# Pooled attention and a two-layer mixer on one core: lambda and alpha1 loaded to all partitions, in place of spreading them by products

## The chip, the core and the metric

The kernel runs on one core of a Trainium2 chip. The metric is the device time of one execution in microseconds (us), the median of several runs. The core has five engines with instruction streams of their own: TensorE (PE; its weight loads are shown apart as PEld), VectorE (DVE), ScalarE (ACT), GpSimd (POOL) and SyncE (SP). SP and ACT issue transfers on hardware queues (q1 and q10 in the profile), POOL on the software queue (q0), which also converts types on the way. All queues are served by the same 16 DMA engines.

## What is computed

For each of 8 batches and 8 heads, 576 tokens of width 64 attend to 72 keys and values, each the mean of 8 neighbouring ones; the heads side by side make x (576 x 512 per batch). Then a mixer works on x: along the tokens, and along the channels through a hidden layer of 2048.

```python
k_p = k.reshape(B, H, Sp, pool, D).mean(axis=3)   # v_p likewise; pool = 8
attn = softmax(q @ k_p.T / sqrt(D))
x = attn @ v_p                                    # heads side by side: (8, 576, 512)
a1 = alpha1 * x + beta1
tok = einsum('ts,bsd->btd', w_tok, a1)
u = x + lam * tok
a2 = alpha2 * u + beta2
out = u + lam * (maximum(a2 @ w_ch1, 0) @ w_ch2)
```

## The kernel before

All order is written out by hand: the schedule of the framework is off, and each engine works through its instructions in the order of the code. The outermost unit is a block of four token chunks of 128 rows (nine blocks). While PE does the channel mixer of block n (`mlp_A`, then `mlp_B` or `product`), the attention of batch n + 1 and its token mixer (`mix_T`) are put between its products, by lists of due times. Nothing of that part is touched. The change lies in what comes before the first block: the constants, the loads of batch 0, its attention, and the transposes of `w_tok`.

**Folding of the vectors.** The kernel multiplies x by `lamal_bc` = lambda * alpha1 (`att_X` L765 and `rest_X` L758) before the token product; beta1 * lambda is one more row of the moving operand (`bias_row`, L471). So it needs lambda and lambda * alpha1 in all 128 partitions, as `lam_bc` and `lamal_bc`. Before, lambda (two rows), beta1 (two rows) and alpha1 (one row) are loaded as rows of a tile `vecs` (L397, L405). PE spreads a row over the partitions by a product of a row of ones with it in fp32: `spread_lam` (L491, 512 columns, which ACT copies to `lam_bc`), and `spread_al1` twice (L498, 256 columns each, which DVE multiplies by `lam_bc` into `lamal_bc`, L499).

**The first loads.** SP issues half of `rem_raw` (the last 64 tokens of q and k), beta1 and alpha2; ACT issues lambda, the other half of `rem_raw`, alpha1 and beta2; POOL issues, on the software queue and in this order, q of heads 0 to 3, k of heads 0 to 3, v (L300, L295), then k, q and v of heads 4 to 7, `w_tok` (L381, L385) and `w_ch1` (L555). The software queue delivers them in that order.

**Attention of batch 0.** `att_F` transposes q on PE (L589), `att_Frem` the rest of q. `double_k` copies a quarter of k on DVE (L620) and casts the rest of k (L365, L366). `att_K` pools k by 16 products (L632) and 4 on the rest (L638); ACT and then DVE take the two halves out to `kpT` (L648). `att_S` makes the scores and ACT their exponentials; `first_V` pools v; `att_AV` multiplies by v, and DVE divides (L749, L751) into `x_tm`. `att_X` and `rest_X` make `xs`, on POOL or DVE. `double_k`, `cast_rem`, `more_constants` (four memsets, L479 to L482) and the evictions all stand on DVE, in code order.

**Weights of the token mixer.** `setup_wtok(i)` transposes a fifth of `w_tok` on PE (L516), and ACT copies it to `wtT` (L519). `setup_rowsum(i)` adds up its columns on PE (L528), and ACT casts the row into `wtT` (L530). `setup_vectors` transposes beta2 and alpha2 (L503, three small ACT copies). `mix_T(0, 0)` (L801) is the first token product; it needs the first fifth of `wtT`, its sum, and all of batch 0's `xs`. DVE adds x (L805), POOL or DVE multiplies by alpha2 (L811), PE transposes (`mix_uT`, L825), and `mlp_A` (L849) begins.

**Unread products.** `keep_warm(n)` (L792) issues n products of 512 columns whose result nobody reads.

The tile `vecs` lends its place later to scaled `w_ch2` weights; its size per partition stays.

Of the kernel before, what the change touches and what calls it, by code (L numbers as in the profile page):

```python
# [7 lines left out]
FP = mybir.dt.float32  # L8
# [3 lines left out]
ALU = mybir.AluOpType  # L12
AX = mybir.AxisListType

P = 128
SPG = 72
DM = 512
# [171 lines left out]
def direct(  # L189
# [28 lines left out]
    def gp(name):  # L218
        return psA.tile([P, 512], FP, tag="gp", name=name)
# [171 lines left out]

    vecs = const.tile([65, 3, DM], FP, tag="vecs", name="vecs")
    ones_row = const.tile([1, P], FP, tag="ones_row", name="ones_row")
    nc.vector.memset(ones_row, 1.0)

    def load_vector(i, src, queue=nc.scalar):
        queue.dma_start(out=vecs[0:65:64, i], in_=src.unsqueeze(0).to_broadcast((2, DM)))  # L397

    new_batch(0)
    load_vector(0, moe_lam)  # L400
    load_rem(0)
    load_q_bf(0, 0)
    load_k16(0, 0)
    load_vector(1, moe_beta1, nc.sync)
    nc.scalar.dma_start(out=vecs[0:1, 2], in_=moe_alpha1.unsqueeze(0))  # L405
    start = const.tile([1, 2], FP, tag="start", name="start")
# [47 lines left out]
    for i in range(2):  # L454
# [6 lines left out]
    nc.vector.memset(pool_vr, 0.0)  # L461
    nc.vector.memset(vr16, 0.0)
    nc.vector.tensor_scalar(out=pool_v[:, 0:64], in0=pool_main, scalar1=8.0, scalar2=None,
                            op0=ALU.mult)
# [4 lines left out]
    def bias_row(i):  # L469
        p0 = 64 - 64 * i  # L470
        nc.vector.tensor_tensor(out=xs_pool[i][p0:p0 + 1, 4, :], in0=vecs[p0:p0 + 1, 1],  # L471
                                in1=vecs[p0:p0 + 1, 0], op=ALU.mult)

# [4 lines left out]
    def more_constants():  # L478
        nc.vector.memset(ones_bf, 1.0)  # L479
        nc.vector.memset(ones_lo[0:64], 1.0)  # L480
        nc.vector.memset(ones_lo[64:128], 0.0)
        nc.vector.memset(wtT[:, :, S:640], 0.0)  # L482

    def load_al2(behind):
        behind.memset(al2_bc[:, 0:1], 0.0)
        nc.sync.dma_start(out=al2_bc, in_=moe_alpha2.unsqueeze(0).to_broadcast((P, DM)))

    def spread_lam():

        ps = gp("ps_bc")  # L490
        nc.tensor.matmul(out=ps, lhsT=ones_row, rhs=vecs[0:1, 0])  # L491
        nc.scalar.copy(out=lam_bc, in_=ps)

    def spread_al1(half):

        ps = gp("ps_bc")[:, 0:256]
        cols = slice(256 * half, 256 * half + 256)
        nc.tensor.matmul(out=ps, lhsT=ones_row, rhs=vecs[0:1, 2, cols])  # L498
        nc.vector.tensor_tensor(out=lamal_bc[:, cols], in0=lam_bc[:, cols], in1=ps, op=ALU.mult)  # L499

# [287 lines left out]
    def keep_warm(count):  # L788

        ps = psB.tile([P, DM], FP, tag="ch", bufs=2, name="ps_warm")  # L790
        for _ in range(count):
            nc.tensor.matmul(out=ps, lhsT=warm[:, 0:P], rhs=warm)  # L792
# [209 lines left out]
    cast_rem(0, nc.vector)  # L1002
    more_constants()
    keep_warm(1)
    att_Frem(0, nc.scalar.copy)
    keep_warm(1)
    spread_lam()
    double_k(0)
    att_K(0, 0, None)
    spread_al1(0)  # L1010
    bias_row(0)
# [6 lines left out]
    att_S(0, 3)  # L1018
    att_AV(0, 1)
    att_K(0, 1, nc.scalar.copy)  # L1020
    att_F(0, 2, nc.vector.tensor_copy)
    late_copy = att_F(0, 3, None)
    att_AV(0, 2)
    att_X(0, 0, 2, nc.gpsimd, False)
    att_AV(0, 3)
# [8 lines left out]
    att_S(0, 6)  # L1034
    spread_al1(1)
    att_AV(0, 5)
# [4 lines left out]
    load_rem(1, behind=nc.vector)  # L1041
    keep_warm(1)
    setup_wtok(1, nc.scalar.copy)
    keep_warm(1)
    att_AV(0, 7)
    keep_warm(1)
    setup_rowsum(0)
    setup_wtok(2, nc.scalar.copy)
    rest_X(0, 4, 6, nc.gpsimd)
    load_w1(1)  # L1050
    setup_wtok(3, nc.scalar.copy)
    setup_rowsum(1)
    setup_vectors()
    setup_wtok(4, nc.scalar.copy)
# [199 lines left out]
```

## Time and profile before

| what | us |
|---|---|
| median of 3 runs (332.32 to 332.98) | 332.51 |
| the profiled execution | 332.4 |
| its span in the profile | 330.7 |
| PE busy | 325.0 |
| DVE / ACT / POOL busy | 236.6 / 175.6 / 95.4 |

The page gives, for one execution, each engine's busy time and the chain of work that ended last. The chain is followed back from the last instruction: at each step to what released it, or to the instruction before it on its engine. A step on the chain counts with the time by which the chain moves on; the timeline counts an instruction's whole duration, which with pipelined products is longer. "Landing" is the time from a DMA's issue to the last update of its semaphore, and the trace has it for POOL's DMAs alone. The view by stages gives each engine's busy time, the granted clock and the GB/s moved in stretches of the span.

### The profile page before, as it was taken

The numbers are of one execution on the slowest core, as the hardware profiler recorded it, in microseconds if no ns is written. First come the engines' busy times: TensorE is split into PE (matmuls) and PEld (weight loads), VectorE is DVE, ScalarE is ACT, GpSimd is POOL, SyncE is SP. The second block draws the span as 40 slices with busy tenths as digits, with TensorE's granted clock in tenths as the row PEclk, the third lists the DMA queues.
The fourth block names the chain that finished last, engine by engine and source line by source line (L and its number), as shares of the span: only waits on it lengthen the run. The fifth ranks groups of instructions, "written<-read, shape, count | busy, mean of one in ns | idle before, by whom it ended". The sixth has DMA issues, their size and how long they took to land.

```text
span 330.7 us, 6526 instructions
## 1 busy us (share of the span) xinstructions
PE 325.0 (98%) x2531; PEld 209.1 (63%) x2531; DVE 236.6 (72%) x490; ACT 175.6 (53%) x322; POOL 95.4 (29%) x110
## 2 busy tenths in 40 slices
PE   8999999999999999999999999999999999999995
PEld 3667764455545576656775677557755866586584
DVE  7774389999589969776967696878688783265263
ACT  3775989368323852387128812782268225803710
POOL 8769736501256011700290028102610200000000
PEclk9999999999999999999999999999999999999999
DMA  8999999958895982399549934995340044003003
GB/s 122 185 218 265 268 209 249 219 145 114 171 258 65 227 199 60 74 235 162 161 116 205 171 122 89 211 196 152 65 136 2 0 65 143 2 0 128 3 32 97
DMA packets 66618, 45.83 MB, mean 139 GB/s; under 512 B 34541, under 2 KB 57205, under 8 KB 66586
## 3 DMA queue, kind: packets, MB, share of 16 engines
q1 hardware_dynamic: 52236, 32.67, 42.4%
q0 software_dynamic: 13824, 12.40, 23.3%
q8 instruction: 20, 0.33, 0.4%
q10 hardware_dynamic: 526, 0.34, 0.4%
q14 instruction: 12, 0.10, 0.1%
HBM read 38.30 MB, written 9.44 MB: 144 GB/s over the span
## 4 chain that ended last, share of the span: by engine, by line
PE 97%; DVE 1%; POOL 0%; issue 0%; ACT 0%
PE ps_h L849 38%; PE ps_w L972 26%; PE ps_tok L801 11%; PE ps_ch L869 8%; PE ps_av L743 3%; PE ps_s L700 2%; PE ps_warm L792 2%; PE ps_kp L632 1%; PE ps_r L707 1%; PE ps_av L747 1%; PE ps_q L589 1%; PE ps_sc L680 0%; PE ps_w L516 0%; DVE u_sb L805 0%; POOL u_bf L811 0%; PE ps_v L659 0%
## 5 line engine op out<-in xcount | busy, mean ns | idle before, releaser
L849 PE MATMUL ps_h<-u_fm,w 128*128 128x512 bf16 (+2 forms) x608 | 133.7, 369 | 0.2 <-DVE bias_cols L852 0.2
L856 ACT ACTIVATE H<-ps_h,bias_cols 128x512 bf16<-128x512 f32 x144 | 98.2, 688 | 55.4 <-PE ps_h L849 54.5
L849 PEld LDWEIGHTS <-w 128*128 128x128 bf16 x608 | 65.8, 114 | 49.7 <-issue 2.2
L972 PEld LDWEIGHTS <-H 128*128 128x128 bf16 x560 | 53.4, 98 | 10.8 <-DVE u_sb L990 1.2
L809 ACT CAST u_bf<-u_sb 128x512 bf16<-128x512 f32 x32 | 19.8, 618 | 71.2 <-issue 39.9
L972 PE MATMUL ps_w<-w_l,H 128*128 128x256 bf16 x448 | 53.6, 273 | 0.0
L990 DVE TENSOR_TENSOR u_sb<-u_sb,ps_w 128x512 f32<-128x512 f32 x54 | 36.2, 682 | 17.1 <-PE ps_w L972 17.1
L765 POOL TENSOR_TENSOR xs<-x_tm,lamal_bc 128x512 bf16<-128x512 f32 x12 | 15.9, 1328 | 108.2 <-DVE x_tm L751 108.0
L801 PE MATMUL ps_tok<-xs,wtT 128*128 128x512 bf16 (+3 forms) x200 | 44.9, 381 | 0.0
L805 DVE TENSOR_TENSOR u_sb<-x_tm,ps_tok 128x512 f32<-128x512 f32 (+1 forms) x40 | 27.3, 683 | 10.0 <-PE ps_tok L801 10.0
L751 DVE TENSOR_TENSOR x_tm<-ps_av,recs 128x320 f32<-128x320 f32 x64 | 31.5, 491 | 2.6
L729 ACT ACTIVATE ET<-ps_s 72x512 f16<-72x512 f32 x56 | 32.3, 591 | 0.0
L801 PEld LDWEIGHTS <-wtT 128*128 128x128 bf16 (+3 forms) x200 | 17.3, 100 | 16.0 <-issue 1.1
L749 DVE RECIPROCAL recs<-ps_av 128x5 f32<-128x5 f32 x64 | 12.1, 188 | 16.7 <-PE ps_av L747 16.3
L670 DVE TENSOR_TENSOR v_u<-v_u 72x1024 f32<-72x1024 f32 (+1 forms) x24 | 22.7, 947 | 0.2
L972 PE MATMUL ps_w<-w_t,h_s 128*128 128x256 bf16 x168 | 22.6, 273 | 0.0
L869 PEld LDWEIGHTS <-H 128*128 128x128 bf16 x128 | 11.9, 98 | 13.7 <-issue 0.4
L372 POOL TENSOR_TENSOR k_raw<-k_raw 128x512 f32<-128x512 f32 x14 | 18.7, 1338 | 2.7 <-DMA k_raw<-in_k_dram 2.6
L374 POOL TENSOR_TENSOR k_bf<-k_raw 128x512 bf16<-128x512 f32 x14 | 18.8, 1343 | 1.1
L972 PEld LDWEIGHTS <-h_s 128*128 128x128 bf16 x168 | 16.4, 98 | 4.1
L941 DVE TENSOR_TENSOR H<-H,H 128x1024 bf16<-128x1024 bf16 x14 | 9.6, 689 | 13.0 <-ACT H L856 13.0
L743 PEld LDWEIGHTS <-ET 72*128 72x128 f16 x256 | 13.9, 97 | 6.4 <-issue 0.3
(153 smaller groups left out, 370.7 us busy)
## 6 DMA issues: line engine op xcount, KB each, us to landing
out_dram<-u_sb SPq DMA_DIRECT2D x29, 256.0 KB
k_raw<-in_k_dram SPq DMA_DIRECT2D x12, 512.0 KB
v_u<-in_v_dram SPq DMA_DIRECT2D x12, 512.0 KB
q_bf<-in_q_dram POOLq DMA_DIRECT2D x16, 256.0 KB, 7.2
w<-in_moe_w_ch_dram POOLq DMA_DIRECT2D x6, 512.0 KB, 14.3
out_dram<-u_sb SPq DMA_DIRECT2D x11, 128.0 KB
w<-in_moe_w_ch_dram POOLq DMA_DIRECT2D x1, 1024.0 KB, 14.4
k_raw<-in_k_dram POOLq DMA_DIRECT2D x2, 512.0 KB, 16.9
```

The source lines that it names most:

```text
L670: nc.vector.tensor_tensor(out=out, in0=t[:, :, 0:width], in1=t[:, :, width:2 * width], op=ALU.add)
L729: nc.scalar.activation(out=o, in_=i, func=AF.Exp, bias=0.0, scale=0.125)
L743: nc.tensor.matmul(out=av[:, odd + c, :], lhsT=ET[:, m0:m0 + 128], rhs=vp1[:, h % 4, :])
L751: nc.vector.tensor_tensor(out=x[:, 1 - odd:6 - odd, dd:dd + D], in0=av[:, :, 0:64], in1=rec.unsqueeze(2).to_broadcast((P, 5, D)), op=ALU.mult)
L801: nc.tensor.matmul(out=ps_tok[p0:p1], lhsT=wtT[0:kk, at, P * c:P * c + p1 - p0], rhs=xs_pool[i][0:kk, sc, :], start=(sc == 0), stop=(sc == 4))
L805: nc.vector.tensor_tensor(out=s["u"][p0:p1, :], in0=x[p0:p1, 1 + c if c < 4 else 5 - 5 * i, :], in1=ps_tok[p0:p1, 0:DM], op=ALU.add)
L809: nc.scalar.copy(out=s["u_bf"], in_=s["u"])
L849: nc.tensor.matmul(out=ps_h[:, t0:t1 + one], lhsT=w1_of(cc, j), rhs=rhs, start=(cc == 0), stop=(cc == 3))
L856: nc.scalar.activation(out=H4[n, j // 4][:, j % 4, :], in_=ps_h, func=AF.Relu, bias=bias_cols[:, j:j + 1], scale=1.0)
L869: nc.tensor.matmul(out=ps, lhsT=H_of(n, j)[:, 128 * m:128 * m + 128], rhs=(w2l if n else w2)[j // 4][:, j % 4, :], start=(j == 0), stop=(j ...
L972: nc.tensor.matmul(out=ps, lhsT=stat(j), rhs=moving(j), stop=(j == 7), start=(first and (pp == 0 or alone) and j == 0), skip_group_check=True)
L990: nc.vector.tensor_tensor(out=o, in0=o, in1=banks[key, "both"], op=ALU.add)
```

## The change

Lambda goes to all 128 partitions of `lam_bc` as SP's first load, and alpha1 to all 128 partitions of `vecs[:, 0]` as ACT's first; each writes 256 KB from a source of 2 KB. One product on DVE, behind the memsets and ahead of `pool_v`, makes `lamal_bc`. `spread_lam` and both `spread_al1` go, with their evictions on ACT and DVE, and so do the row of ones and its memset. `more_constants` moves behind the eviction of pooled k. Ahead of `att_K(0, 0)` stand two unread products (one before), behind it one more; the three between the transposes of `w_tok` go. `setup_vectors` moves ahead of the second `att_K`, `att_AV(0, 2)` and its `att_X` ahead of the transposes of the second q, and `setup_wtok(2)` ahead of the first row sum.

```diff
-    def load_vector(i, src, queue=nc.scalar):
-        queue.dma_start(out=vecs[0:65:64, i], in_=src.unsqueeze(0).to_broadcast((2, DM)))
+    vecs = const.tile([P, 3, DM], FP, tag="vecs", name="vecs")
     new_batch(0)
-    load_vector(0, moe_lam)
+    nc.sync.dma_start(out=lam_bc, in_=moe_lam.unsqueeze(0).to_broadcast((P, DM)))
+    nc.scalar.dma_start(out=vecs[:, 0], in_=moe_alpha1.unsqueeze(0).to_broadcast((P, DM)))
     load_rem(0)
     load_q_bf(0, 0)
     load_k16(0, 0)
-    load_vector(1, moe_beta1, nc.sync)
-    nc.scalar.dma_start(out=vecs[0:1, 2], in_=moe_alpha1.unsqueeze(0))
+    nc.sync.dma_start(out=vecs[0:65:64, 1], in_=moe_beta1.unsqueeze(0).to_broadcast((2, DM)))
...
     nc.vector.memset(vr16, 0.0)
+    nc.vector.tensor_tensor(out=lamal_bc, in0=lam_bc, in1=vecs[:, 0], op=ALU.mult)
     nc.vector.tensor_scalar(out=pool_v[:, 0:64], in0=pool_main, scalar1=8.0, scalar2=None,
...
-                                in1=vecs[p0:p0 + 1, 0], op=ALU.mult)
+                                in1=lam_bc[p0:p0 + 1], op=ALU.mult)
...
     cast_rem(0, nc.vector)
-    more_constants()
     keep_warm(1)
     att_Frem(0, nc.scalar.copy)
-    keep_warm(1)
-    spread_lam()
+    keep_warm(2)
     double_k(0)
     att_K(0, 0, None)
-    spread_al1(0)
+    keep_warm(1)
+    more_constants()
     bias_row(0)
...
     att_AV(0, 1)
+    setup_vectors()
     att_K(0, 1, nc.scalar.copy)
+    att_AV(0, 2)
+    att_X(0, 0, 2, nc.gpsimd, False)
     att_F(0, 2, nc.vector.tensor_copy)
     late_copy = att_F(0, 3, None)
-    att_AV(0, 2)
-    att_X(0, 0, 2, nc.gpsimd, False)
...
     att_S(0, 6)
-    spread_al1(1)
     att_AV(0, 5)
     att_X(0, 4, 6, nc.gpsimd, False)
     att_S(0, 7)
     setup_wtok(0, nc.scalar.copy)
     att_AV(0, 6)
     load_rem(1, behind=nc.vector)
-    keep_warm(1)
     setup_wtok(1, nc.scalar.copy)
-    keep_warm(1)
     att_AV(0, 7)
-    keep_warm(1)
+    setup_wtok(2, nc.scalar.copy)
     setup_rowsum(0)
-    setup_wtok(2, nc.scalar.copy)
     rest_X(0, 4, 6, nc.gpsimd)
     load_w1(1)
     setup_wtok(3, nc.scalar.copy)
     setup_rowsum(1)
-    setup_vectors()
     setup_wtok(4, nc.scalar.copy)
```

More of the change, by code (lines that the diff above doesn't have):

```diff
@@ L390, in direct @@
     b2row = const.tile([8, P], FP, tag="b2row", name="b2row")
-    vecs = const.tile([65, 3, DM], FP, tag="vecs", name="vecs")
-    ones_row = const.tile([1, P], FP, tag="ones_row", name="ones_row")
-    nc.vector.memset(ones_row, 1.0)
-    def load_vector(i, src, queue=nc.scalar):
-        queue.dma_start(out=vecs[0:65:64, i], in_=src.unsqueeze(0).to_broadcast((2, DM)))
+    vecs = const.tile([P, 3, DM], FP, tag="vecs", name="vecs")
     new_batch(0)
-    load_vector(0, moe_lam)
+    nc.sync.dma_start(out=lam_bc, in_=moe_lam.unsqueeze(0).to_broadcast((P, DM)))
+    nc.scalar.dma_start(out=vecs[:, 0], in_=moe_alpha1.unsqueeze(0).to_broadcast((P, DM)))
     load_rem(0)
@@ L486, in load_al2 @@
         nc.sync.dma_start(out=al2_bc, in_=moe_alpha2.unsqueeze(0).to_broadcast((P, DM)))
[L488 to L499, printed above, removed]
     def setup_vectors():
```

## The prediction, on record before the result was known

> **What bounds the kernel now.** First I read the page's shares and the chain that ended last.
>
> ```profile
> PE 325.0 (98%) x2531; PEld 209.1 (63%) x2531; DVE 236.6 (72%) x490; ACT 175.6 (53%) x322; POOL 95.4 (29%) x110
> ...
> PE 97%; DVE 1%; POOL 0%; issue 0%; ACT 0%
> ```
>
> PE is busy nearly throughout and is 97% of the chain. From about 27.6 us, where the channel mixer begins, I take the rest as a fixed tail of PE work: what the start gains or loses by then arrives at the end. So the sum is made for the first 28 us alone. Second, the chain from 17 to 28 us, in order of time (start, length, what):
>
> ```profile
> 17.10 0.62 PE ps_bc L498 x2
> ...
> 18.29 0.47 PE ps_w L516 x5
> 18.76 0.12 PE ps_av L743 x4
> 18.88 0.03 PE ps_av L747
> 18.91 0.22 PE ps_warm L792
> 19.13 0.28 PE ps_w L516 x5
> 19.41 0.22 PE ps_warm L792
> 19.63 0.12 PE ps_av L743 x4
> 19.75 0.03 PE ps_av L747
> 19.78 0.22 PE ps_warm L792
> 20.00 0.28 PE ps_rs L528 x5
> ...
> 21.11 0.15 PE ps_vec L503
> 21.27 0.28 PE ps_w L516 x5
> 21.55 1.19 PE ps_tok L801 x5
> ```
>
> On paper it is PE without a gap, so that each product taken out would be a gain. But a chain that runs through an engine without a gap doesn't say what else was just in time. So third, the timeline of the weight loads at 18.29, the first transpose of `w_tok`:
>
> ```profile
> 18.29 0.30 PEld L516 LDWEIGHTS <-wt_bf 128*128 128x128 bf16 x5 [0.24 <-DMA wt_bf<-in_moe_w_tok_dram]
> ```
>
> It was released by the transfer of `w_tok`. The view of that tile gives issue at 8.3 and 9.9 us to landing, 18.2 us: PE and the transfer arrive there together. I call this point the gate. Fourth, the view by stages (stretch, its length, busy time of PE, PEld, DVE, ACT and POOL, clock, DMA share in us, GB/s):
>
> ```profile
> 2.00:3.00 1.00, 1.00 (x3) 0.30 (x2) 0.89 (x4) 0.00 (x0) 1.00 (x2) 1.00 0.24 68
> 3.00:4.00 1.00, 1.00 (x4) 0.38 (x3) 0.99 (x5) 0.11 (x1) 0.88 (x3) 1.00 0.58 50
> 4.00:6.00 2.00, 2.00 (x6) 0.68 (x5) 0.95 (x5) 1.38 (x2) 1.93 (x6) 1.00 1.35 210
> 18.00:20.00 2.00, 1.99 (x29) 1.41 (x28) 1.66 (x7) 1.87 (x4) 1.26 (x2) 1.00 1.12 214
> 20.00:22.00 2.00, 2.00 (x29) 1.59 (x27) 1.93 (x5) 1.72 (x5) 1.30 (x3) 1.00 1.09 263
> ```
>
> The software queue works through its loads without a pause from 4 us on, at about 200 GB/s. The start has two bounds that meet at the gate: PE's products, and the transfers.
>
> **PE's sum, if nothing else bound it.** Ahead of the gate, on the chain: `spread_lam` 1.05 us (7.82 to 8.87) and the second `spread_al1` 0.62 go; one more unread product ahead of pooled k costs 0.22 (the length of such a product on the chain); `setup_vectors`, 0.15, comes here from behind the gate. The first `spread_al1` (two passes, 0.69 from 9.46) runs beside the evictions of pooled k (ACT 9.57 to 9.97, DVE 10.00 to 10.47), so it gains nothing, and the unread product put in its place costs nothing while those 0.9 us stand. That is -1.05 - 0.62 + 0.22 + 0.15 = -1.30. Behind the gate: three unread products, 3 x 0.22 = 0.66, and `setup_vectors`, 0.15: -0.81. Together -2.11 us.
>
> **Ahead of the gate: the transfers.** PE can't pass the gate before `w_tok` has landed, so the -1.30 becomes a wait, and the gate moves only with the landing. What the change does to that: two loads write 128 x 2 KB each, 262 KB, together 524 KB, ahead of nearly all others. Nothing moves before 2.25 us (0 GB/s). From there to 4.0 the engines move 118 KB now (68 and 50 in a us each). The trace has one load of the same form, alpha2 (SP, issued 16.46, seen by its effect at 20 to 22): with it the total rises from 214 to 263 GB/s. At 263 the time from 2.25 to 4.0 has room for 460 - 118 = 342 KB, so that 182 of the 524 KB remain to compete with the software queue. Price of competing: in 20 to 22 alpha2's 262 KB leave the others 526 - 262 = 264 KB, where 428 were moved in 18 to 20: 164 KB less, at 214 GB/s 0.77 us for one such load. So the slip of the gate is 182 / 262 x 0.77 = 0.53 us. Bounds: 0, if all of it fits into the idle start; 1.54, if both loads compete in full. I take 0.55, since the idle stretch is seen and the rate in it is the doubtful part.
>
> [...]
>
> **The same loads on the hardware queues.** `rem_raw` now stands behind them. The cast of the rest of q started at 6.45 and that of the rest of k at 7.92 with no wait shown, so they had landed. Estimate: by the sum above alpha1 is through at about 4.7, and the four 64 KB parts follow; with the last of them about 1 us later than now, at some 8.9, its casts end 0.7 later, the last 4 products of pooled k end at 9.8 instead of 9.55. So pooled k is not sooner; it is bound by the casts, though the 1.05 us of `spread_lam` are gone. PE then comes to the gate at 18.29 + 0.25 - 0.62 + 0.15 = 18.07, still ahead of the landing at 18.8. The later loads keep to their order: the second q landed at 13.6 (used 13.81), v at 15.0 (15.09); they slip as the gate does, and PE waits there already. It has no further effect, since 0.62 go between them and the gate. `att_AV(0, 2)` put ahead of that q covers 0.15 of it.
>
> **DVE and ACT.** The new product on DVE has the size of L765's, 0.69 us. DVE stood idle for 1.05 us before `pool_v` (4.55 to 5.60, waiting for POOL), which hides it if alpha1 has landed by 4.9; later, it costs 1 us for 1, up to where `rem_raw` is late anyway (6.8 by the estimate), so 0. `more_constants` (6.92 to 7.69) stands after the eviction of pooled k, ahead of `bias_row` and the eviction of v. Before, the half product for `lamal_bc` (0.42) stood there; 0.35 more against an idle time of 0.38 ahead of the v eviction at 12.00: hidden, without that cover 0.35. `setup_vectors`' three copies on ACT (0.31, from 22.24 to 22.55) now stand ahead of the eviction of the second pooled k, beside the transposes of q: 0 to 0.2, ahead of the gate, so without effect. ACT's 0.59 copy of `lam_bc` and its chain go too.
>
> **Behind the gate: -0.81 of PE, of which DVE lets through 0.36.** `mix_T(0, 0)` also needs `xs` of the last heads, on DVE:
>
> ```profile
> 19.18 0.49 DVE L751 TENSOR_TENSOR x_tm<-ps_av,recs 128x320 f32<-128x320 f32 x1
> 19.63 0.06 DVE L332 MEMSET rem_raw<- 128x4 f32 x1
> 19.82 0.19 DVE L749 RECIPROCAL recs<-ps_av 128x5 f32<-128x5 f32 x1
> 20.04 0.49 DVE L751 TENSOR_TENSOR x_tm<-ps_av,recs 128x320 f32<-128x320 f32 x1
> 20.57 0.69 DVE L765 TENSOR_TENSOR xs<-x_tm,lamal_bc 128x512 bf16<-128x512 f32 x1
> ```
>
> With no unread products ahead of `att_AV(0, 7)` the reciprocal moves up from 19.82 only to DVE's free time, 19.71: 0.11. `xs` is then ready at 21.26 - 0.11 = 21.15, and with 0.04 of release the token product starts at 21.19 instead of 21.55. PE alone would be there at 20.74. ACT's copies of `wtT` (the row sum's cast now third in line, done 2.8 us behind the gate) come within the first four products. Behind this, u, the product with alpha2 and its transposes follow `mix_T` as before; alpha2 itself lands with the 20 to 22 stretch and has over 1 us.
>
> **Sum:** +0.55 - 0.36 = +0.2 us on the profiled execution's 332.4 (span 330.7 and 1.7 around it): 332.6. That execution is 0.1 under the median of 332.51, inside the runs' own 0.66, so I don't correct for it. By the bounds of the slip: 332.4 - 0.36 = 332.0, and 332.4 + 1.54 - 0.36 = 333.6. A measurement of this kernel can tell 0.2%, 0.66 us, from no change; the forecast is a tie.
>
> **Rivals.**
> - *The queue yields more (slower).* If the two loads don't use the idle start, for want of descriptors or because the first issue takes long (ACT's first issue took 1.14 us), they compete in full with q, k and v. Place: landing of `w_tok`; price up to 1.54 - 0.36 = +1.2, 333.6. It decides once the slip passes 1.02 us. For it: the software queue, too, moves only 50 KB from 3 to 4 us, so something other than traffic holds the start. Against: those 2 us are seen idle.
> - *`rem_raw` far behind.* If the last of it lands after about 9.75 us rather than 8.9, PE reaches the gate after `w_tok`; at 10.5, +0.4 over the forecast, 333.0. Part of the slower cases where it adds up with the slip.
> - *The products were the bound (faster).* If the landing doesn't bind, or comes no later and DVE's path is shorter than I read, PE's whole sum arrives: 332.4 - 2.1 = 330.3. For it: the chain has no gap at all. Against: the wait at 18.29 names the transfer, and landing and start agree to 0.1 us.
> - *The clock.* The first 13 unread products took 5.44 us, 0.42 each, those at 7.3 and later 0.22. If PE's new waits brought the slow pace back, a few us of products would double. The waits are under 1 us each; I give it nothing of its own.
>
> **Chances.** Slip of 0 to 1.02 us, the tie: 0.55, with 331.9 to 333.06 as its own range. Slip over 1.02, or `rem_raw` with it: 0.28. PE's sum in whole or in its greater part: 0.17, between 330.3 and 331.7. The range leaves about 0.12 below and 0.06 above: 331.7 to 333.6.
>
> **What would show it.** Right: PE waits at the first transpose of `w_tok` for the transfer, by over 0.5 us; `w_tok` lands at about 18.8; the token product starts some 2.9 us behind the gate instead of 3.26; pooled k is made no earlier. Wrong: `w_tok` lands where it did or over 1 us later; the token product waits for something other than DVE; a waiting time appears behind 28 us.

## The result and the profile after

| | before | after |
|---|---|---|
| median of 7 runs each | 332.51 us | 334.8 us |
| lowest to highest | 332.0 to 334.32 | 334.09 to 335.55 |
| ratio of the times, 95% interval | | 1.0059 [1.0034, 1.0083] |
| the profiled execution (its span) | 332.4 (330.7) | 335.55 (333.8) |
| PE busy | 325.0 | 323.0 |

The change made the kernel slower by 2.3 us, and the forecast of 332.6 with a range up to 333.6 missed it. PE works 2.0 us less, about as predicted, and yet the end comes later. The page of the changed kernel, busy times and chain:

```profile
PE 323.0 (97%) x2524; PEld 208.3 (62%) x2524; DVE 237.4 (71%) x488; ACT 174.8 (52%) x321; POOL 96.8 (29%) x110
...
PE 91%; DVE 4%; DMA 2%; issue 1%; POOL 1%; ACT 0%; POOLq 0%
```

Before, PE alone was 97% of the chain. Now a transfer stands on it and DVE has four times its share: the work that was only just covered has come through. Where it does so, the chain says in order of time (start, length, what):

```profile
2.27 7.71 DMA k<-in_k_dram
9.98 0.05 issue
10.03 0.82 PE ps_kp L615 x16
...
11.95 0.17 DVE ones_bf L475
12.11 0.13 DVE ones_lo L476
...
12.49 0.22 DVE wtT L478
...
12.74 0.68 DVE xs L467
...
13.46 0.43 DVE vp L647
...
15.96 0.49 DVE x_tm L734
16.45 0.34 DVE qT L579
16.79 0.04 issue
16.83 0.38 PE ps_sc L663 x2
```

The chain starts with the landing of the first k, 7.71 us behind its issue, where it took 5.4 before. Then come DVE's `more_constants` and `bias_row` (11.95 to 13.42), ahead of the eviction of v, and a third pair of values (`x_tm`, 15.96) ahead of the copy of the second q, for which the scores of head 4 wait. PE's own waits, and the gate of the prediction, in the timelines of products and of weight loads:

```profile
8.43 0.62 PE L572 MATMUL ps_q<-identity_bf,q_bf 128*128 128x128 bf16 x8 [1.86 <-DMA q_bf<-in_q_dram]
...
16.83 0.38 PE L663 MATMUL ps_sc<-qT,kpT 128*72 128x256 bf16 x2 [0.54 <-DVE qT L579]
```

```profile
19.45 0.34 PEld L499 LDWEIGHTS <-wt_bf 128*128 128x128 bf16 x5
```

The last line is the first weight load from `w_tok`, and it has no wait any more: the first part of `w_tok` landed at 18.43 (18.25 before), PE came at 19.5. The gate held nothing. Set instruction against instruction, PE stood later than before by 1.76 us at the first transposes of q, 1.39 at the end of pooled k, 2.25 at the scores of head 4, 1.23 at the first transposes of `w_tok`, 0.93 at the first token product and 0.92 at 27.6 us. There it stayed up to 61 us. At 70 us it was 2.45, and from there 2.4 to the end. (This execution lost 0.8 more behind the last product, where SP's issue of two stores took 2.03 us; before it was 1.13.)

So there are two losses: 0.9 us in the first 22 us, and 1.5 us between 61 and 70, in a stretch that the change doesn't touch.

**The first loss begins in the queues.** The DMA view for 2 to 6 us, in 40 slices of 0.1 us: busy share of the 16 engines in tenths, and GB/s. The kernel before:

```profile
DMA  0010034761334900164999999999999999999999
GB/s 0 0 41 0 0 97 113 225 174 31 56 46 51 56 0 5 26 56 41 159 179 200 195 174 164 205 215 195 215 210 210 205 195 236 267 261 251 210 241 174
```

The changed kernel:

```profile
DMA  0377799989987884452223696765898999999999
GB/s 20 123 287 287 307 369 410 369 307 348 430 328 307 307 272 159 169 149 67 82 97 103 205 179 113 133 103 97 123 128 128 138 123 138 143 169 148 179 164 205
```

With the two loads in front the engines move some 290 to 430 GB/s from 2.2 to 3.4 us. As the prediction had it, the bytes use the idle start, and faster than its 263. But the start was not free. Before, the software queue moved its first packets at 3.0 us, slowly (38 and 56 in the two half microseconds from there, then 156), and from 3.9 on the engines are full. After, its first packet is at 4.33, the same slow beginning follows (58 and 103 packets in the half microseconds from 4.5), and 200 GB/s are reached at 6 us. What looked idle was the time in which that queue got going (3.0 to 3.9 us), and the loads pushed it back. q landed at 8.38 instead of 6.13, k at 9.98 instead of 7.64, the two v at 11.24 and 11.63 instead of 9.22 and 9.64; the second k, q and v 0.9, 0.7 and 0.7 later; the first part of `w_tok` 0.18.

This is not the chance of one execution. In six profiles with the first loads of the kernel before (before, e3, e4, e5, e11, e16 below) the software queue's first packet came at 3.00 to 3.04 us, q landed at 6.03 to 6.71 and k at 7.64 to 8.19. In the ten with those of the changed kernel (after, e6, e7, e9, e12 to e15, e17, e18) it was 3.70 to 4.50, 7.81 to 9.12 and 9.37 to 10.67. For `w_tok` the two overlap: 17.71 to 18.70 and 17.85 to 20.41.

**The second loss, 61 to 70 us.** POOL sums up the k of batch 2, and DVE scales `w_ch2`. Kernel before, POOL and then DVE:

```profile
56.87 1.28 POOL L372 TENSOR_TENSOR k_raw<-k_raw 128x512 f32<-128x512 f32 x1 [2.13 <-DMA k_raw<-in_k_dram]
...
60.01 1.26 POOL L372 TENSOR_TENSOR k_raw<-k_raw 128x512 f32<-128x512 f32 x1 [0.51 <-DMA k_raw<-in_k_dram]
```

```profile
61.03 3.68 DVE L908 TENSOR_TENSOR w_l<-w,lam_bc 128x512 bf16<-128x512 bf16 x4
```

Changed kernel, the same groups, and the product of PE that waits for DVE behind them:

```profile
58.67 1.27 POOL L372 TENSOR_TENSOR k_raw<-k_raw 128x512 f32<-128x512 f32 x1 [3.01 <-DMA k_raw<-in_k_dram]
...
62.63 1.73 POOL L372 TENSOR_TENSOR k_raw<-k_raw 128x512 f32<-128x512 f32 x1 [1.34 <-DMA k_raw<-in_k_dram]
64.43 1.59 POOL L374 TENSOR_TENSOR k_bf<-k_raw 128x512 bf16<-128x512 f32 x1
```

```profile
61.94 4.63 DVE L891 TENSOR_TENSOR w_l<-w,lam_bc 128x512 bf16<-128x512 bf16 x4
```

```profile
70.02 2.32 PE L832 MATMUL ps_h<-u_fm,w 128*128 128x512 bf16 x10 [1.37 <-DVE ps_ch L858]
```

The second k is there 2.6 us later, though all around it is only 0.9 later. So POOL's second pair of operations runs beside DVE's four products; one of these took 0.68 us alone and up to 1.75 beside POOL, and POOL's own went from 1.27 to 1.59 and 1.73. Why both took longer isn't shown. DVE then reaches the evictions of `ps_ch` too late for PE. The k came late while the transfers were slow, in the view by stages of 55 to 60 us (last column: GB/s), before and then after:

```profile
55.00:60.00 5.00, 5.00 (x24) 2.25 (x23) 4.67 (x8) 4.50 (x9) 2.55 (x2) 1.00 1.16 210
```

```profile
55.00:60.00 5.00, 5.00 (x25) 2.25 (x23) 4.93 (x9) 5.00 (x9) 1.93 (x2) 1.00 1.13 137
```

The engines were as busy (a share of 1.16 and 1.13), with a packet of 2 KB (the loads of v, from 57 us on some stores of the output too) taking 252 ns on average instead of 158. The packets of k itself, 1 KB each, took 120 to 171 ns by the microsecond from 55 us on, where it was 87 to 101 before.

### The profile page after: what moved, and what is told of

It reads as the page before. It is cut to its first block, busy times and chain, and to the rows that moved or that the text cites. A ratio compares the mean times of both kernels' runs of the same rounds, so it can differ in the third digit from the quotient of the medians.

```text
span 333.8 us, 6510 instructions
## 1 busy us (share of the span) xinstructions
PE 323.0 (97%) x2524; PEld 208.3 (62%) x2524; DVE 237.4 (71%) x488; ACT 174.8 (52%) x321; POOL 96.8 (29%) x110
## 4 chain that ended last, share of the span: by engine, by line
PE 91%; DVE 4%; DMA 2%; issue 1%; POOL 1%; ACT 0%; POOLq 0%
PE ps_h L832 38%; PE ps_w L955 26%; PE ps_tok L784 11%; PE ps_ch L852 6%; PE ps_av L726 2%; PE ps_s L683 2%; DMA k<-in_k_dram 2%; DVE w_l L891 2%; DVE u_sb L788 1%; PE ps_kp L615 1%; PE ps_r L690 1%; PE ps_av L730 1%; PE ps_w L499 0%; POOL u_bf L794 0%; PE ps_rs L511 0%
```

## The experiments

One table for all, from each kernel's profile: landing of the first q and k; how much later than in the kernel before the first token product started; the slip of PE's products at 50 to 58 us; mean time of a 2 KB packet at 55 to 60 us; start of POOL's second sum; the slip from 80 us on. Last, the median of the runs and the ratio to the runs of the kernel before on the same chip.

| kernel | q, k land | token | at 50 | packet ns | 2nd sum | at 80 | median | ratio |
|---|---|---|---|---|---|---|---|---|
| before | 6.13, 7.64 | 0 | 0 | 158 | 60.01 | 0 | 332.51 | |
| after | 8.38, 9.98 | +0.9 | +0.92 | 252 | 62.63 | +2.4 | 334.8 | 1.0059 [1.0034, 1.0083] |
| e1 loads added | 6.91, 8.96 | +2.1 | +2.12 | 184 | 59.86 | +2.1 | 336.99 | 1.0156 [1.0112, 1.02] |
| e2 loads behind rest | 7.21, 10.25 | +1.2 | +1.30 | 174 | 59.98 | +1.2 | 335.46 | 1.007 [1.0036, 1.0104] |
| e3 no late unread | 6.71, 8.19 | +0.2 | +0.16 | 212 | 60.93 | +0.9 | 332.84 | 0.9994 [0.9973, 1.0016] |
| e4 order only | 6.03, 7.68 | +0.5 | +0.51 | 175 | 60.45 | +0.5 | 333.66 | 1.0028 [1.0007, 1.0048] |
| e5 before, scale later | 6.44, 7.95 | -0.3 | -0.25 | 204 | 60.52 | +1.7 | 334.8 | 1.0067 [1.0044, 1.009] |
| e6 after, scale later | 7.81, 9.41 | +0.4 | +0.66 | 197 | 60.78 | +4.1 | 337.19 | 1.0123 [1.0088, 1.0159] |
| e7 after, more unread | 8.96, 10.40 | +1.4 | +1.36 | 241 | 62.69 | +2.5 | 334.33 | 1.004 [1.002, 1.0061] |
| e8 distinct rows | 7.39, 9.30 | +1.0 | +0.99 | 183 | 60.61 | +0.9 | 337.33 | 1.0105 [1.0057, 1.0153] |
| e9 loads, old order | 8.10, 9.45 | +1.0 | +1.04 | 207 | 62.49 | +2.1 | 333.81 | 1.003 [1.0002, 1.0058] |
| e10 half loads | 6.84, 8.43 | +4.0 | +3.98 | 159 | 61.73 | +3.9 | 336.82 | 1.0109 [1.0069, 1.0149] |
| e11 order, pair back | 6.63, 8.11 | +2.4 | +2.37 | 191 | 60.87 | +2.3 | 332.94 | 1.0002 [0.9975, 1.0029] |
| e12 e7 + k first | 9.00, 10.49 | +1.9 | +1.85 | 222 | 65.67 | +4.9 | 336.2 | 1.0092 [1.006, 1.0124] |
| e13 after, pair back | 9.12, 10.67 | +2.2 | +2.17 | 233 | 62.41 | +2.4 | 333.74 | 1.0039 [1.0021, 1.0058] |
| e14 e7 + pair back | 8.67, 10.03 | +0.6 | +0.68 | 240 | 62.65 | +2.5 | 334.52 | 1.0045 [1.0018, 1.0072] |
| e15 e7 + v later | 7.83, 9.37 | +0.3 | +0.23 | 165 | 59.17 | +0.2 | 332.75 | 1.0022 [0.9999, 1.0046] |
| e16 before, v later | 6.42, 7.97 | +0.2 | +0.14 | 173 | 59.98 | +0.1 | 332.81 | 1.0015 [1.0003, 1.0027] |
| e17 three remedies | 7.92, 9.54 | +1.0 | +0.92 | 216 | 61.38 | +1.3 | 332.77 | 1.0009 [0.9982, 1.0036] |
| e18 after, v later | 7.92, 9.52 | +0.5 | +0.51 | 223 | 61.53 | +1.3 | 334.27 | 1.0053 [1.0028, 1.0078] |

A profile is one execution, and a column can show what only that one had: e1, e9, e10, e11 and e13 were taken with the half clock told of below in the first 20 us, e6 with it from 77.5 to 80.9 us.

### The loads by themselves: e1, e2, e8, e10

e1 is the kernel before with the two loads put first and nothing taken out; their tiles are overwritten later:

```diff
     new_batch(0)
+    nc.sync.dma_start(out=lam_bc, in_=moe_lam.unsqueeze(0).to_broadcast((P, DM)))
+    nc.scalar.dma_start(out=lamal_bc, in_=moe_alpha1.unsqueeze(0).to_broadcast((P, DM)))
     load_vector(0, moe_lam)
```

> The kernel before with one thing added: the two 256 KB loads of lambda and alpha1 to all partitions, first on SP's and ACT's queues; they go into lam_bc and lamal_bc, which the products then overwrite as before, so nothing of the result changes. Theory Q (the loads hold back the software queue's first packets): q lands at about 8.3 us instead of 6.1, k at about 10 instead of 7.6, pooled k ends at about 10.9 instead of 9.55, and as nothing is taken out in return the channel mixer begins 1.4 to 1.6 us later: 334 us, ratio 1.004 or more. Rival O (the new order costs, not the loads): within 0.3 us of the kernel before, 332.5 to 332.8.

It is 4.5 us slower by the medians (4.0 without its two longest runs), though `w_tok` landed at 17.35, earlier than before. Part is the later q and k: 0.8 and 1.3 us against the kernel before, not the 2.2 and 2.4 that theory Q named. The greater part is the clock, as e8 below shows: with q and k even later, it takes 333.35 at full clock, in two runs.

The same two loads thus hold q back less here than in the changed kernel (6.91 against 8.38). Behind them ACT issues its halves of `rem_raw` (128 KB) at 2.42 and 3.06 us here, and at 1.26 and 1.94 in the changed kernel, where no row of lambda stands ahead of them. That these halves then hold back the software queue, too, would fit; no run tests it.

The clock shows in e1's view by stages (the third column from the right):

```profile
6.00:7.00 1.00, 0.19 (x2) 0.05 (x2) 0.51 (x3) 0.95 (x2) 1.00 (x3) 1.00 1.34 217
7.00:8.00 1.00, 0.79 (x9) 0.46 (x9) 0.00 (x0) 0.61 (x2) 1.00 (x2) 1.00 1.37 217
8.00:9.00 1.00, 0.46 (x4) 0.20 (x4) 0.69 (x4) 0.60 (x2) 1.00 (x3) 1.00 1.45 205
...
11.00:12.00 1.00, 0.88 (x6) 0.38 (x5) 0.75 (x2) 0.54 (x2) 1.00 (x2) 0.92 1.44 195
12.00:13.00 1.00, 1.00 (x8) 0.89 (x7) 0.81 (x2) 0.83 (x4) 0.51 (x2) 0.50 1.46 196
13.00:14.00 1.00, 1.00 (x5) 0.25 (x4) 0.00 (x0) 0.22 (x1) 0.26 (x1) 0.50 1.47 223
14.00:15.00 1.00, 1.00 (x10) 0.79 (x10) 0.65 (x2) 0.53 (x2) 0.00 (x0) 0.50 1.13 227
15.00:16.00 1.00, 1.00 (x26) 0.94 (x25) 0.85 (x4) 0.89 (x3) 0.00 (x0) 0.87 1.06 217
```

PE, without work for half of the time from 6 to 9 us, got half the clock from 11.85 to 15.26, 3.41 us. What brings it on isn't shown: PE was busy for 57% and 93% of the two stretches of 3.41 us before it, and in the changed kernel's profile it was busy for 45% of the 3.41 us from 5.98 and kept the full clock (1.00 there and up to 15.2 us). All six runs of e1 had a mean clock of 0.975 to 0.995. Its price can be read from the kernel before: over the five groups of experiments 105 of its runs had a mean clock of 0.998 or more, median 332.47, and 19 had less, median 334.35. That is 1.9 us.

e2 is the changed kernel with the loads behind `rem_raw` on their queues and the product for `lamal_bc` behind `double_k(0)`:

```diff
-    nc.sync.dma_start(out=lam_bc, in_=moe_lam.unsqueeze(0).to_broadcast((P, DM)))
-    nc.scalar.dma_start(out=vecs[:, 0], in_=moe_alpha1.unsqueeze(0).to_broadcast((P, DM)))
     load_rem(0)
+    nc.sync.dma_start(out=lam_bc, in_=moe_lam.unsqueeze(0).to_broadcast((P, DM)))
+    nc.scalar.dma_start(out=vecs[:, 0], in_=moe_alpha1.unsqueeze(0).to_broadcast((P, DM)))
```

> The changed kernel with the two loads moved behind the four parts of rem_raw on their queues, and the product for lamal_bc moved behind the casts of the rest of k, where DVE waits for ACT. Theory Q: the software queue starts as in the kernel before, q lands at 6.1 to 6.4, k at 7.6 to 8.2, pooled k ends at 8.8 to 9.4, and the time falls to 332.0 to 332.7, with the landing of w_tok (18.3 to 19.3) as the next bound. Rival O: the order stays, so the loss stays, 334 or more. If the loads cost by their bytes wherever they stand, w_tok lands at 19 or later and the time is 333 to 333.5.

335.46 against the 334.8: the place ahead of `rem_raw` is not the cause, and theory Q's 332.0 to 332.7 was missed. Here the software queue began at 3.04, but was then thinned out: 21 to 80 packets in each half microsecond from 6.0 to 8.0, where 127 to 194 were moved before. The loads cost the first q and k time at either place.

e8 asks whether it matters that one row is read 128 times. It is e1 with 128 different rows as the source:

```diff
-    nc.sync.dma_start(out=lam_bc, in_=moe_lam.unsqueeze(0).to_broadcast((P, DM)))
-    nc.scalar.dma_start(out=lamal_bc, in_=moe_alpha1.unsqueeze(0).to_broadcast((P, DM)))
+    nc.sync.dma_start(out=lam_bc, in_=moe_w_ch2[0:P, :])
+    nc.scalar.dma_start(out=lamal_bc, in_=moe_w_ch2[P:2 * P, :])
```

> The kernel before with two loads of 256 KB first on the two hardware queues, as in e1, but from 128 different rows of a weight instead of one row read 128 times. Theory E (the bytes and packets delay the first software loads): q lands near 6.9 and k near 9.0 as in e1, the token product comes about 1 to 2 us later than in the kernel before, and the median is 334.4 to 337. Theory F (it is the one row read 128 times over): the two loads end sooner than 3.7 to 5.2, q lands at 6.1 to 6.4 and k at 7.6 to 8.0, and the median is 332.5 to 333.

The rows came in faster (397 GB/s from 2.5 to 3.5 us, all through by 4.0), and q and k were late by 1.3 and 1.7 all the same. Theory E holds for the landings, F falls. The two runs at a clock of 0.998 or more took 333.35 and 333.36; the others, at 0.985 or less, 337.3 and more.

e10 is e1 with 64 partitions (`lam_bc[0:64]`, `lamal_bc[0:64]`) instead of 128.

> The kernel before with two loads of 64 partitions instead of 128 (128 KB each), first on the two hardware queues, unread until overwritten: half of the bytes of e1. Theory L (what counts is how long the loads hold the DMA engines at the start): half the delay, q at 6.4 to 6.7, k at 8.0 to 8.5, the token product 0.3 to 1.0 us later than before, median 332.9 to 334.0. Rival N (it is the place of one load ahead of rem_raw and its fixed latency, not the bytes): the same landing as in e1, 6.9 and 9.0. Rival Z (up to some size the loads fit into the idle start): q at 6.1 and k at 7.7, median 332.5.

q 0.7 and k 0.8 later, for half the bytes; e1 had 0.8 and 1.3. With the 0.6 us by which both vary among the six profiles of the old start, that says little on how the delay grows with the bytes. `rem_raw` was later than in e1 (the first transposes of the rest of q +1.8 against the kernel before, +1.2 in e1), all six runs had a clock of 0.983 to 0.989, and the time says nothing on the dose: 336.82, where theory L had 332.9 to 334.0.

### The order by itself: e3, e4, e11, e13

e3 takes the three late unread products out of the kernel before, and nothing else:

```diff
-    keep_warm(1)
     setup_wtok(1, nc.scalar.copy)
-    keep_warm(1)
     att_AV(0, 7)
-    keep_warm(1)
```

> The kernel before without the three unread products between the transposes of w_tok, nothing else. By the prediction's step behind the gate DVE lets 0.36 us of the 0.66 through: the first token product starts at about 21.2 instead of 21.55, 332.15 us. If PE alone binds there: -0.66, 331.85. If the transfers bind again behind the gate, or the products kept a pace that now falls: no change or slower.

No difference that can be measured in the times. In its profile the step behind the gate is there: the first token product starts 2.89 us behind the first transposes of `w_tok`, where it was 3.19. But in that execution `w_tok` landed 0.45 later, PE waited for it, and the second loss came on top (+0.16 at 50 us, +0.9 at 80): a kernel with the old first loads has it, too.

e4 is the changed kernel with the old small loads, `spread_lam` and `spread_al1` put back (`spread_lam` in place of one of the two unread products, `spread_al1(0)` in place of the one behind pooled k), so that only the order is new.

> The changed kernel with the kernel before's small loads and fp32 products put back (spread_lam in place of one unread product, the first half of alpha1 in place of the other), so that only the new order and the missing late unread products are left of the change. Theory Q: q and k land as in the kernel before, pooled k ends at 9.4 to 9.6, and the time is that of the kernel before less up to 0.4: 332.1 to 332.6. Rival O: most of the loss stays, 333.5 to 334.8.

1.15 us slower than the kernel before, with q and k landing as before. DVE's timeline of e4, and PE's at the scores of head 4:

```profile
14.38 0.19 DVE L749 RECIPROCAL recs<-ps_av 128x5 f32<-128x5 f32 x1
14.60 0.49 DVE L751 TENSOR_TENSOR x_tm<-ps_av,recs 128x320 f32<-128x320 f32 x1
15.01 0.41 DVE L596 COPY qT<-ps_q 128x512 bf16<-128x512 bf16 x1
```

```profile
15.48 0.38 PE L680 MATMUL ps_sc<-qT,kpT 128*72 128x256 bf16 x2 [0.54 <-DVE qT L596]
```

Before, the copy of the second q began at 14.10, ahead of that reciprocal. `att_AV(0, 2)` put in front gives DVE two instructions that PE's next scores don't need, ahead of one that they do. e11 puts this pair back:

```diff
-    att_AV(0, 2)
-    att_X(0, 0, 2, nc.gpsimd, False)
     att_F(0, 2, nc.vector.tensor_copy)
     late_copy = att_F(0, 3, None)
+    att_AV(0, 2)
+    att_X(0, 0, 2, nc.gpsimd, False)
```

> The order alone (e4) with the third pair of values put back behind the two transposes of the second q. Theory V (in e4 the pair's reciprocal and product on DVE went ahead of the copy of the second q, so that PE waited for that copy): the score product of head 4, +0.90 in e4, comes at most 0.2 us later than before, the token product at most +0.2, median 332.3 to 332.9 (ratio 0.999 to 1.001). If the other moves of the order (vectors ahead of pooled k, row sum behind) cost: the token product stays at +0.5, median 333.2 to 333.7.

332.94, ratio 1.0002. Its profile says nothing on this (half clock from 11.3 to 18.1, q late by 0.5 already). At a clock of 0.998 or more, e11 has 8 runs with a median of 332.66 and e4 has 10 with 333.62. So this one move costs about 1 us here, and the rest of the new order next to nothing (the kernel before has 332.47 at full clock). e13 makes the same edit in the changed kernel:

> The changed kernel with the third pair of values put back behind the two transposes of the second q. Theory V (the pair in front makes PE wait for DVE's copy of the second q, as in e4 against e11): the score product of head 4 comes at +1.3 to +1.5 against the kernel before instead of +2.25, the token product at +0.3 to +0.7 instead of +0.9, and the median falls to 334.0 to 334.4. Rival (PE arrives late there anyway, since k was late; the order has no further effect): token product at +0.9, median 334.8.

333.74, 1.1 us less than the changed kernel's 334.8 (the intervals still overlap) and a little under the 334.0 to 334.4 of theory V. Again the profile fell on a run with half the clock (9.0 to 12.4). With e7's unread products added, the same edit brings nothing that shows: 334.33 and 334.52 (e7, e14), 332.75 and 332.77 (e15, e17), all below. So the 1 us isn't a price that every version pays.

### The clock: e7

```diff
-    keep_warm(13)
+    keep_warm(18)
...
-    keep_warm(2)
+    keep_warm(4)
     double_k(0)
```

> The changed kernel with 18 instead of 13 warm products ahead of q, and 4 instead of 2 ahead of k. Theory C (part of the loss is a clock that falls to half after PE has waited for q and k): the mean clock of each run is 0.998 or more, no slice of the first 20 us shows a clock of 0.5, and the median is 334.0 to 334.5, below the changed kernel's 334.8. Theory D (the loss is the later landing and the new order, whatever the clock): the median stays within 0.3 of 334.8, and the added products (0.22 us each at most) push K no later, since k lands later than they end.

All 12 runs had a clock of 0.998 or more, where the changed kernel had 4 of 7 below (0.992 to 0.995). The median is 0.5 us lower, but the intervals overlap, and the changed kernel's runs at full clock (334.09, 334.8, 335.55) are no faster than the others. So the clock is at most a small part of this change's loss; in e1 and e8 it is most of it. The runs of e7 spread from 332.76 to 335.21 at full clock: something else varies between executions.

### The second loss: e5, e6, e12, e15, e16

e5 (before) and e6 (after) move the four `scale_w2` products behind POOL's sums:

```diff
-            for piece, at in enumerate((13.9, 15.3, 19.2, 19.4, 24.5, 24.9, 25.3, 25.7, 26.9, 27.9)):
+            for piece, at in enumerate((13.9, 15.3, 19.2, 19.4, 31.2, 31.3, 31.4, 31.5, 26.9, 27.9)):
```

> The kernel before with the four scale_w2 products moved from due 24.5-25.7 to 31.2-31.5 of block 0, behind the ps_ch evictions of the next batch. Theory A (the second loss of the changed kernel is DVE's four scale_w2 products running beside POOL's sums of k and holding the ps_ch evictions): in the kernel before this pair already overlaps in part (3.68 us for four that take 0.68 each alone), so the gain here is 0 to 0.5 us: 332.0 to 332.5. Theory B (the order there is nothing but what the landing of k_raw makes it; DVE's products don't matter): 332.5, ratio 1.000. If DVE's pushed work is late for the v sums: 333 to 333.5.

> The changed kernel with the same move of scale_w2. Theory A: PE no longer waits 1.4 us for the ps_ch eviction near 69 us, the slip against the kernel before stays at +0.9 from the token product to the end, and the median falls by some 1.5 us, to 333.3 (ratio 1.002 to 1.003). Theory B: POOL's sums themselves are late (the later k_raw), so the slip still rises to +2.4 near 69 us and the median stays at 334.8 (ratio 1.006 to 1.007).

In e6 PE's slip indeed didn't rise near 69 us: +0.66 at 50 and at 70. But the products pushed back stood in the way of the sums of v, PE waited 1.8 us for DVE there, and with the half clock of that execution behind it the slip was +4.1 at 80; e5, at full clock, lost 2 us in the same place. Theory A has its mechanism, not its gain: DVE has no room for these products later on.

e12 (on e7) issues batch 2's k ahead of its rest of q and k (`12.91` to `12.87`):

> The changed kernel with the added warm products (e7, whose runs all kept a clock of 0.998 or more and yet spread from 332.8 to 335.2) and with batch 2's two loads of k issued ahead of its rest instead of behind it. Theory K (the second loss, near 67 us, is the late landing of the second of these loads): it lands before 61 us, POOL's second sum starts before 61, the slip near 67 us doesn't rise by more than 0.5, and the runs gather at 332.8 to 333.6. Rival M (the slow packets of that stretch, 240 to 250 ns each against 158 before, take their time in any order): the rest of q and k lands late instead, POOL waits for that, the slip rises by 1.5 as in e7, and the median stays at 334.0 to 334.5.

Worse. In POOL's code the casts of the rest stand ahead of the sums of k; the first cast waited 6.43 us, and the second sum began at 65.67:

```profile
61.43 0.40 POOL L357 CAST rem_q<-rem_raw 128x256 bf16<-128x256 f32 x1 [6.43 <-DMA rem_raw<-in_q_dram]
```

Rival M was right here: what is put behind is late instead. e15 (on e7) and e16 (on before) issue the loads of v of batch 2 later, so that k should have the engines more to itself:

```diff
-                    at = 13.21 + 0.01 * u if b == 1 else (6.7 if b == 2 else 3.5) + 4.0 * u
+                    at = 18.0 + 0.01 * u if b == 1 else (6.7 if b == 2 else 3.5) + 4.0 * u
```

> The changed kernel with the added warm products of e7 and with the gate of batch 2's first two loads of v on DVE some 5 us later, so that they start about 2.5 us later and batch 2's k comes in with less beside it. Theory K (the second loss is the late landing of the second load of k, made late by slow packets beside the loads of v): POOL's second sum starts before 61 us, the slip near 67 us doesn't rise by more than 0.5, the runs gather at 332.8 to 333.6. Rival M (the packets are slow whatever stands beside them, or v comes late in place of k, at 70 us): median 334.0 to 335.

> The kernel before with the same later v of batch 2, as a control of e15. Theory K: 332.3 to 332.7, since k lands in time there already. If v is then late for its sums at 70 us: 333 to 334, and e15 has to be read against this.

e15's POOL and DVE:

```profile
56.07 1.27 POOL L372 TENSOR_TENSOR k_raw<-k_raw 128x512 f32<-128x512 f32 x1 [1.00 <-DMA k_raw<-in_k_dram]
...
59.17 1.27 POOL L372 TENSOR_TENSOR k_raw<-k_raw 128x512 f32<-128x512 f32 x1 [0.47 <-DMA k_raw<-in_k_dram]
```

```profile
61.26 2.89 DVE L891 TENSOR_TENSOR w_l<-w,lam_bc 128x512 bf16<-128x512 bf16 x4
```

The second sum starts at 59.17, the four products take 2.89, and the slip doesn't rise: +0.23 at 50, +0.16 at 80. 332.75 against e7's 334.33, with 8 of the 12 runs at 332.1 to 333.2 and 4 at 334.4 to 335.3; the intervals of the two overlap a little. The control e16 lost 0.3. Theory K's first half holds: where the second k comes in time, the second loss is absent. Its second half, that the loads of v make k slow, isn't shown. The issue of v moved from 49.00 to 50.79 us (e7, e15) and from 47.65 to 50.71 (before, e16), but its first packet hardly: 53.87 and 53.36, 53.41 and 53.36. In e15 as in e7 some 50 packets of v had started by 55 us, so the edit did not clear the engines for k, and why e15's packets were faster stays open.

### The loads in the old order: e9, e14

e9 is the kernel before with the loads in place of the products (an unread product for `spread_lam` and for `spread_al1(0)`) and every other step where it was.

> The loads without the new order: the kernel before with the two broadcast loads in place of the small ones, without the fp32 products (an unread product in the place of two of them), all other steps and the late unread products where they were. Theory L (the loads' delay of q and k is the greater part, the order adds its own loss): q lands near 8.4 and k near 10.0 as in the changed kernel, the token product comes 0.4 to 1.0 us later than before, and the median is 333.3 to 334.3, that is the changed kernel's 334.8 less the 0.5 to 1.2 that the order alone cost. Theory S (the loads cost the same with either order, the order adds nothing once PE waits for k anyway): within 0.3 of 334.8. If the products taken out pay for the later landing: 332.5.

333.81: theory L. Of its 7 runs at full clock 5 are at 332.3 to 333.2 and two at 334.3 and 335.3. By these five the products taken out nearly pay for the later landing; that the two others had the second loss would fit, but no profile shows it.

> The changed kernel with the added warm products of e7 and the pair put back as in e13, so that neither a slow clock nor the order is left, only the later landing and the slow stretch near 55 to 61 us. If the three causes add up: all clocks at 0.998 or more, median 333.2 to 334.0 (e7 gave 334.33), with the fastest runs at 332.3. If only the later landing counts: 334.3 as e7.

e14 has e7's unread products and e13's order. Full clock in all 7 runs, and a token product only 0.6 late, yet a median of 334.52: its profile has the second loss at its dearest, +0.68 to +2.5. The causes don't add up, and the table says how they combine. Leave out e5, e6 and e12, which reorder that stretch. Where the slip rose behind 61 us (after, e3, e7, e9, e13, e14, e17, e18), the start of POOL's second sum less the slip at 80 is 60.0 to 60.4 us in every row; where it did not, it is 57.8 to 60.0. So the end is as late as the later of two things: PE as it left the start, or the second sum less some 60.2 us. In the five profiles whose second sum starts between 62.4 and 62.7 us (after, e7, e9, e13, e14) the end is 2.1 to 2.5 late, whether PE came there with 0.68 or with 2.17: what is lost at the start is not lost again at 61 us.

### All remedies, and the later v alone: e17, e18

> The changed kernel with all three remedies: the added warm products (e7), the third pair of values behind the second q (e13) and the later loads of v (e15). If the three causes are what the change lost by, beside the later first landing: all clocks at 0.998 or more, most runs at 332.0 to 332.6, median within 0.3 of the kernel before (332.1 to 332.7), not more than a few runs above 334. If the later landing of q and k costs PE time that nothing gives back: 333.3.

> The changed kernel with nothing but the later loads of v of batch 2. Theory K (the second loss is that of k behind slow packets beside v): the median falls by 1.0 to 1.6 against the changed kernel's 334.8, to 333.2 to 333.8, with no rise of the slip near 67 us; runs with a clock under 0.998 remain 1 to 2 us above. Rival M: 334.5 to 335.

e17 (e7, e13 and e15 together) is back at the kernel before: 332.77, ratio 1.0009 [0.9982, 1.0036]. With the loads in and the products out there is no further cause of that size. It is not better either; of its 12 runs 5 lie above 333.9. e18 gives 334.27, less gain than the 1.0 to 1.6 of theory K, and its interval overlaps the changed kernel's. Of its 12 runs 7 had a clock below 0.998; the five others have a median of 333.69, inside theory K's range, so the clock may hide part of what the edit did. In the profiles of both, packets took 216 and 223 ns again and the second sum came at 61.4 to 61.5. So with v issued later the slow stretch is still there. No version beat the kernel before.

## Why the prediction was wrong

- **"PE's sum"** was right in size: PE's busy time fell by 2.0, its -2.11.
- **"Ahead of the gate: the transfers"** priced the loads at the gate, 0.53 us; `w_tok` slipped 0.18, inside its bounds. The step failed in where it looked. The delay of the software queue was largest at its first loads, 2.3 us at q and k, and nearly made up by its eighth, the first part of `w_tok`. (The second part, its ninth, landed 1.4 later, at 19.82, but PE needs it only at 21.93.) The prediction measured the delay where it had almost gone.
- **"The same loads on the hardware queues"** is the step that lost the first 0.9 us. It let `rem_raw` alone be late, kept q and k where they were, and had pooled k end at 9.8. It ended at 10.95, bound by k itself. PE so came to the gate at 19.5, not 18.07, and the gate became harmless. The view by stages quoted there (50 GB/s at 3 to 4 us) was read as an idle stretch, and the rival "the queue yields more" even named the doubt: something other than traffic holds the start. It then put that rival's price, too, at the landing of `w_tok`.
- **"DVE and ACT"**: `more_constants` was called hidden in 0.38 us of idle time, with 0.35 as its price without cover. With k late the cover was gone; it stands on the chain with `bias_row`, 11.95 to 13.42. And `att_AV(0, 2)`, which was to cover 0.15 us of the slip, costs about 1 us where the loads are the old ones (e4 against e11): the sum counted PE's products and not the two instructions on DVE that came with them, ahead of the copy of q.
- **"Behind the gate: -0.81 of PE, of which DVE lets through 0.36"** was about right: the token product starts 2.89 us behind the first transposes of `w_tok` (19.52 to 22.41), as predicted, where it was 3.19 (18.29 to 21.48), so 0.30 were gained back.
- **"A fixed tail of PE work" from 27.6 us** is the step that lost the other 1.5 us, at 61 to 70. POOL already waited 0.51 us for k there and then ran beside DVE's products, where one of these took 1.75 us for 0.68 and POOL's last operation 1.60 for 1.28; with k 2.6 us late, two of the products took 1.75 us, and the second sum 1.73 instead of 1.26. The shift of 0.9 by itself isn't the cause: e1, e2, e8 and e10 came there 1.0 to 4.0 late and lost nothing. What the changed kernel's profile had on top was slow packets, and what brings these on stays open.
- **"The clock. ... I give it nothing"**: the wait for q was 1.9 us, not under 1 us. The half clock came in 4 of 7 runs by their mean clock. It makes most of the loss of e1 and e8; in the changed kernel it is not shown to have made the median worse (e7, at most 0.5).

Open is why the packets of 55 to 60 us take 240 to 250 ns in the profiles of some kernels and 160 to 180 in others. The profiles with the loads of v issued later had 165 to 223, two with the old first loads (e3, e5) 212 and 204; issue times alone don't sort them. Which part of the spread between runs at full clock it makes isn't shown, since a profile catches one run.

## What to carry to other kernels

Price a transfer put ahead of a queue at the first consumer of that queue, not at the last: here the first loads, q and k, landed 2.3 us later and the eighth, the first part of `w_tok`, 0.18. A stretch in which engines look idle can be the time in which a queue gets going, as here from 3.0 to 3.9 us. And when a step is moved up, count its evictions on the other engines: two short instructions ahead of a copy that PE waits for cost about 1 us here (e4 against e11). Where two delays meet at one point, the later one alone counts, so that taking away the other brings nothing.

## What was not expected of the hardware

- In the kernel before, the software queue moved 38 and 56 packets in the first two half microseconds from its first packet, then 156; with the two loads on the other queues in front, that beginning moved back from 3.0 to 4.33 us in the two profiles shown, and came at 3.7 to 4.5 in ten.
- Packets of 2 KB took 158 to 252 ns each in the same stretch of different kernels, at nearly the same busy share of the DMA engines (1.16 and 1.13 in the kernel before and the changed one, which are the ends), with 210 and 137 GB/s there.
- A DVE product of a bf16 tile and `lam_bc` (128 x 512), 0.68 us alone, took up to 1.75 beside an addition on POOL, which itself went from 1.27 to 1.73.
- Half the clock for 3.41 us came behind about 1.6 us of idle time of PE within 3 us in e1, while a wait of 1.9 us in one piece (6.56 to 8.43) led to none in the changed kernel's profile; runs of the kernel before with a lowered clock are 1.9 us longer by the medians.
